# Phases of two key steps with eight slots, two streams of half contractions and an MLP that goes chunk by chunk, in a fused attention and MLP kernel

## The chip, the cores and the metric

The kernel runs on one core of a Trainium2 chip. The metric is the device time in microseconds (us) of one execution, lower is better; before the change the median of three runs is 1293.92 us (1293.52 to 1295.2).

## The reference

Per token a gate `g` mixes an attention output and an MLP output. The attention has 32 query heads of 16 channels that share one key and one value head; the MLP has a hidden width of 1792 and a squared ReLU. There are 2048 tokens of width 512, all in float32.

```python
g = sigmoid((x * gate_w).sum(-1, keepdims=True))
q = (x @ wq).reshape(B, S, 32, 16).transpose(0, 2, 1, 3)
p = softmax(einsum("bhqd,bkd->bhqk", q, x @ wk) * 16 ** -0.5)
a = einsum("bhqk,bkd->bhqd", p, x @ wv).transpose(0, 2, 1, 3).reshape(B, S, 512) @ wo
h = relu(x @ w1 + b1) ** 2
b = h @ w2 + b2
out = g * a + (1 - g) * b
```

## The kernel before

**Numbers.** A float32 factor is cut into a rounded part `r` and a rest `l` (a *split*: two VectorE instructions, a cast L163 and a subtraction L164), and a product of two factors is three matrix products (`pairs`, L166). A matmul with a contraction of 128 is done as two halves of 64 rows that run side by side on the array, each into a PSUM bank of its own; `mm2` (L173) issues the two halves of a term in a row. Such a pair is called a *slot* here. VectorE adds the two banks when the last term is in. There are three banks for this (`mp`), four for scores (two tiles of two banks, `sp`) and one for the context (`acc`).

**Attention.** The tokens are cut into four chunks `c` of 512, the heads into eight groups of four: 32 iterations `it` (chunk by chunk). An iteration goes over 16 key tiles of 128 (*steps*). A step is two *half-steps* of 256 queries: `scores` (L496) issues two matmuls side by side (L503) and the exponential of their 128x1024 results on ScalarE (L507), into a buffer `e`. `context` (L510) multiplies the exponentials with the values and a column of ones (L518): four matmuls side by side in 32 columns each, with 512 queries where both halves of a step are at hand, otherwise with 256. `finish` (L535) copies the sums out; `unpack` (L186) moves them by two DMAs of SP's queue, `q_load` (L355) loads the queries of the next iteration by six more, and `pieces` (L553) divides them on VectorE in four parts of 128 columns (`divide`, L526) and stores `oTs`.

**The other work.** `work` (L605) is a generator that yields between slots: 14 tiles of query projection (`qproj`; the first two are done ahead of the attention), the MLP, and the output projection. The MLP (`mlp`, L438) goes over pairs of hidden tiles `f`, and within a pair over the four chunks: `first` (L440) makes a hidden tile (12 slots; bias, square and split on VectorE, L449 to L451), `second` (L456) adds two hidden tiles to the result `res[c]` (four units of 6 slots, two evictions L468 each). All `x` chunks and all of `res` stay in SBUF; each weight tile is loaded (`w_load`, 512 KB for both layers) and split (`w_split`) once, in three buffers.

**The order is written out by hand.** `phase` (L657) issues one piece of division, one *chore* of the list `chores` (a load, a split, or nothing), and then scores of three half-steps with six slots among them (`FULL`), or of two half-steps with two slots (`LIGHT`, three in the last unit); then follows the context of the phase before. `by_now` (L429) pulls chores forward when a unit needs the weight they split. Which kind comes next is what the generator yields. An iteration of 32 half-steps makes eleven full phases, one of which has two half-steps. All engines work through their own queue in this order.

Of the kernel before, what the change touches and what calls it, by code (L numbers as in the profile page):

```python
# [21 lines left out]
KT = D // 128  # L22
# [12 lines left out]
FULL, LIGHT = 3, 2  # L35
# [4 lines left out]
C_ID, C_BLK, C_A, C_ONE, C_SEL, C_N = 0, 128, 136, 137, 138, 155  # L40
# [15 lines left out]
def exact_shift(tc, k_aug, v_ext, qs, oTs, gms, cs, wo, o_load, o_split, outproj, unpack):  # L56
# [63 lines left out]
    with tc.tile_pool(name="gx", bufs=1) as gx, tc.tile_pool(name="gy", bufs=4, space=PSUM) as gy:  # L120
        wof = gx.tile([128, KT, D], F32, name="wof")
        wor = gx.tile([128, KT, D], F32R, name="wor")
        wol = gx.tile([128, KT, D], F32R, name="wol")
        nc.sync.dma_start(wof, wo.rearrange("(t p) n -> p t n", p=128))
        nc.vector.tensor_copy(wor, wof)
        nc.vector.tensor_tensor(wol, wof, wor.bitcast(F32), OP.subtract)
        for c in range(NC):
            orr, orl, todo = o_split(gx, c, o_load(gx, c))
            for f in todo:
                f()  # L130
            for _ in outproj(gx, gy, c, orr, orl, wor, wol, "gm"):
                pass
# [3 lines left out]
def mix_kernel(ctx: ExitStack, tc: tile.TileContext, xT, wkv, wq, wo, w12, b1, b2, cst, out):  # L136
# [3 lines left out]
    gms = dram.tile([2, 16, 128], F32, name="gms")  # L140
    keep = ctx.enter_context(tc.tile_pool(name="keep", bufs=1))
# [18 lines left out]
    res = []  # L160
# [12 lines left out]
    def mm2(pa, pb, terms, per):  # L173

        for i, (a, b) in enumerate(terms):
            for ps, rows in ((pa, slice(0, 64)), (pb, slice(64, 128))):
                nc.tensor.matmul(ps, a[rows], b[rows], start=i == 0, stop=i == len(terms) - 1)  # L179
            if i < len(terms) - 1:  # L180
                if i % per == per - 1:
                    yield FULL if per > 3 else LIGHT
                elif i % per == 2:
                    yield 0

# [5 lines left out]
    def o_load(xpool, c, n=KT):  # L191
        oT = xpool.tile(sh, F32, name="oT", tag=("xr0", "xl0")[c % 2])
        nc.sync.dma_start(oT[:, :n], oTs[c * NG:c * NG + 2 * n].rearrange("(t u) d n -> (u d) t n", u=2))
        return oT

    def o_split(xpool, c, oT):
        orr = xpool.tile(sh, F32R, name="orr", tag=("xr2", "xr3")[c % 2])
        orl = xpool.tile(sh, F32R, name="orl", tag=("xl2", "xl3")[c % 2])
        return orr, orl, [lambda t=t: split(orr[:, t], orl[:, t], oT[:, t]) for t in range(KT)]

    def outproj(pool, pp, c, orr, orl, wor, wol, tag):
        for j in range(4):
            cols = slice(j * 128, (j + 1) * 128)
            ps = [pp.tile([128, D], F32, name=tag) for _ in range(2)]
            yield from mm2(*ps, [u for t in range(KT) for u in
                                 pairs(orr[:, t, cols], orl[:, t, cols], wor[:, t], wol[:, t])], 2)
            s = 4 * c + j
            ot = pool.tile([128, D], F32, name="ot", bufs=2)
            nc.vector.scalar_tensor_tensor(ot, ps[0], g[:, s:s + 1], res[c][:, j], op0=OP.mult, op1=OP.add)  # L209
            nc.vector.scalar_tensor_tensor(ot, ps[1], g[:, s:s + 1], ot, op0=OP.mult, op1=OP.add)  # L210
            nc.gpsimd.dma_start(out[s * 128:(s + 1) * 128], ot)
            yield LIGHT
# [6 lines left out]
    with fast, tc.tile_pool(name="at", bufs=1) as at, \  # L219
# [5 lines left out]
        wkvf = at.tile([128, KT, 128], F32, name="wkvf", tag="wf")  # L225
# [3 lines left out]
        def x_load(c):  # L229
            for a in range(2):  # L230
                if a == 0:
                    both = at.tile([128, KT, CH], F32, name="xf", tag="e", bufs=3)
# [14 lines left out]
        b2t = at.tile([128, D], F32, name="b2t")  # L247
        nc.sync.dma_start(b2t, bass.AP(tensor=b2.tensor, offset=b2.offset, ap=[[0, 128], [1, D]]))
        nc.sync.dma_start(b1t, b1.rearrange("(t p) -> p t", p=128))

        blk = at.tile([128, 8], BF, name="blk")
        ones = at.tile([96, 128], BF, name="ones")
        wkr = at.tile([128, KT, 128], F32R, name="wkr", tag="w1r", bufs=3)
        wkl = at.tile([128, KT, 128], F32R, name="wkl", tag="w1l", bufs=3)
# [7 lines left out]

        def run(gen):
            while True:
                try:
                    next(gen)
                except StopIteration as e:
                    return e.value
# [8 lines left out]
        def kv(c):  # L277
            ps = mp.tile([128, CH], F32, name="mm")
            mm(ps, [t for k in range(KT) for t in pairs(wkr[:, k], wkl[:, k], xr[c][:, k], xl[c][:, k])])
            kvs = at.tile([128, CH], F32, name="kvs", tag="h", bufs=2)  # L280
            kb = at.tile([128, CH], F32R, name="kb", tag="of", bufs=8)
            sq = at.tile([96, CH], BF, name="sqk", tag="sq", bufs=2)
# [29 lines left out]
        def qproj(c, t, early=False):  # L312
            cols = slice(t * 128, (t + 1) * 128)
            terms = [u for k in range(KT) for u in
                     pairs(wqr[:, k, cols], wql[:, k, cols], xr[c][:, k], xl[c][:, k])]
            qr = at.tile([128, CH], F32R, name="qr", tag="of", bufs=8)
            ql = at.tile([128, CH], F32R, name="ql", tag="of", bufs=8)
            sq = at.tile([128, CH], BF, name="sq", bufs=2)
            if early:
                q = mp.tile([128, CH], F32, name="mm")  # L320
                mm(q, terms)
                nc.scalar.activation(qr, q, AF.Copy)
            else:
                ps = [mp.tile([128, CH], F32, name="mm") for _ in range(2)]
                yield from mm2(*ps, terms, 6)
                q = at.tile([128, CH], F32, name="qf", tag="of", bufs=8)
                nc.vector.tensor_copy(q, ps[0])
                nc.vector.tensor_tensor(q, q, ps[1], OP.add)
                nc.vector.tensor_copy(qr, q)
            nc.vector.tensor_tensor(ql, q, qr.bitcast(F32), OP.subtract)  # L330
            nc.vector.tensor_tensor(sq, qr.bitcast(F32), qr.bitcast(F32), OP.mult)
# [5 lines left out]
            return it, sq  # L337

        def qnorm(it, sq):
            p8 = mp.tile([128, CH], F32, name="mm")  # L340
            nc.tensor.matmul(p8[:8], blk, sq, start=True, stop=True)  # L341
            nrm = at.tile([8, CH], F32R, name="nrm", bufs=2)
            tmp = at.tile([8, CH], F32, name="tmp", tag="n")
            nc.vector.tensor_copy(tmp, p8[:8])
            root(nrm, tmp, tmp)
            o = qs[it, 0, DH]
            nc.sync.dma_start(bass.AP(tensor=o.tensor, offset=o.offset,
                                      ap=[[KS * 2 * CH, 4], [CH, 2], [1, CH]]), nrm.bitcast(F32))
            done.update((it, it + 1))
# [13 lines left out]
        wf, w1, w2 = {}, {}, {}  # L363

        def w_load(f):
            wf[f] = at.tile([128, 1024], F32, name="wf")
            nc.sync.dma_start(wf[f], w12[f])

        def w_split(f, half):

            dst = (w1, w2)[half]
# [397 lines left out]
```

## Time and profile before

| of the profiled execution | |
|---|---|
| its time | 1294.1 us |
| span from first to last instruction | 1292.2 us |
| TensorE matmuls (PE), busy | 1263.2 us, 98% |
| ScalarE (ACT), busy | 1030.8 us, 80% |
| VectorE (DVE), busy | 625.8 us, 48% |
| mean granted TensorE clock | 0.992 |
| DMA | 57.36 MB, mean 44 GB/s |

The profile was taken on the core itself. PE is TensorE's matmuls, PEld its weight loads, which lie beside them; SPq is the queue from which SyncE issues DMAs. A line of a view gives the engine, the line of the kernel, output and inputs by the program's names, the shape, how many there were, their busy time and the mean of one in ns; "idle" or a bracket is the time that the engine stood just ahead, and what ended it. Matmuls overlap, so their busy time says little of how many more would fit; starts of neighbouring instructions say more.

### The profile page before, as it was taken

To read this page: it belongs to the slowest core of one execution; us is meant where nothing else is said; L and a number is where in the kernel's file an instruction comes from. 1 tells how busy PE (TensorE), PEld (TensorE's weight loads), DVE (VectorE), ACT (ScalarE), POOL (GpSimd) and SP (SyncE) were. 2 spreads that over 40 slices of the span, in tenths; PEclk is the share of its full clock that TensorE was granted. 3 is DMA by queue.
4 is the path that set the end of the run, shared out by engine and by line. 5 is a ranking of instruction groups with operands and counts; after the bars stand their busy time and mean duration, and the time that the engine had idled before them with its cause. 6 is when DMAs were issued, how large, how long until landed. Compare 5 with 4: busy or idle time off the path is not lost.

```text
span 1292.2 us, 25244 instructions
## 1 busy us (share of the span) xinstructions
PE 1263.2 (98%) x10722; PEld 642.5 (50%) x10722; DVE 625.8 (48%) x1117; ACT 1030.8 (80%) x1084; POOL 58.9 (5%) x66
## 2 busy tenths in 40 slices
PE   8899999999999999999999999999999999999996
PEld 5455555555555555555555555555554433322232
DVE  6567855546555464464645547457580304020212
ACT  5677787777877777777777777877779999999984
POOL 2010150200000000000000000000000000000000
PEclk9899999999999999999999999999999999999998
DMA  6233311000101000110011000121001120110100
GB/s 207 79 92 90 93 39 38 30 14 34 38 22 47 15 27 26 39 46 15 16 38 38 30 14 33 38 88 62 18 13 39 46 78 31 53 38 22 54 1 35
DMA packets 29661, 57.36 MB, mean 44 GB/s; under 512 B 8936, under 2 KB 10600, under 8 KB 29544
## 3 DMA queue, kind: packets, MB, share of 16 engines
q1 hardware_dynamic: 23288, 44.40, 10.6%
q0 software_dynamic: 5968, 10.77, 2.6%
q8 instruction: 86, 1.41, 0.4%
q10 hardware_dynamic: 288, 0.52, 0.1%
q14 instruction: 31, 0.25, 0.1%
HBM read 31.02 MB, written 16.78 MB: 37 GB/s over the span
## 4 chain that ended last, share of the span: by engine, by line
PE 91%; ACT 5%; DVE 1%; DMA 1%; issue 1%; SPq 0%; ACTq 0%; DVEq 0%
PE acc L518 35%; PE mm L179 30%; PE s L503 23%; ACT e L507 5%; PE mm L171 1%; DMA xf<-in_xT 1%; DMA qa<-qs 1%; PE mm L341 0%; PE s L171 0%; DMA qs<-nrm 0%; DVE res L468 0%; PE mm L568 0%; PE s L300 0%; ACT accs L545 0%; DVE al L541 0%
## 5 line engine op out<-in xcount | busy, mean ns | idle before, releaser
L507 ACT ACTIVATE e<-s 128x1024 f32<-128x1024 f32 x1024 | 998.5, 1024 | 228.4 <-PE s L503 178.9
L518 PE MATMUL acc<-e,v_ext 128*32 128x512 f32 (+1 forms) x5128 | 524.8, 514 | 0.7 <-ACT e L507 0.7
L503 PE MATMUL s<-qa,k_aug 49*128 49x512 f32 x2048 | 452.5, 439 | 13.0 <-ACT e L507 9.5
L503 PEld LDWEIGHTS s<-qa,k_aug 49*128 49x128 f32 x2048 | 193.7, 184 | 329.7 <-ACT e L507 217.2
L518 PEld LDWEIGHTS acc<-e,v_ext 128*32 128x32 f32 x5128 | 129.2, 108 | 223.4 <-issue 194.3
L468 DVE SCALAR_TENSOR_TENSOR res<-mm,omg,res 128x512 f32<-128x512 f32 x224 | 168.2, 751 | 132.7 <-PE mm L179 119.6
L449 DVE TENSOR_SCALAR h<-mm,b1t 128x512 f32<-128x512 f32 x56 | 42.0, 751 | 208.1 <-PE mm L179 208.1
L179 PE MATMUL mm<-w2r,hr 64*128 64x512 f32 x448 | 91.5, 397 | 0.1
L179 PE MATMUL mm<-w2l,hr 64*128 64x512 f32 x448 | 90.3, 392 | 0.0
L179 PE MATMUL mm<-w2r,hl 64*128 64x512 f32 x448 | 89.7, 390 | 0.0
L179 PE MATMUL mm<-xr,w1l 64*128 64x512 f32 x448 | 88.7, 393 | 0.0
L179 PE MATMUL mm<-xr,w1r 64*128 64x512 f32 x448 | 88.2, 391 | 0.0
L179 PE MATMUL mm<-xl,w1r 64*128 64x512 f32 x448 | 88.2, 390 | 0.0
L209 DVE SCALAR_TENSOR_TENSOR ot<-mm,g,res 128x512 f32<-128x512 f32 x12 | 9.0, 752 | 120.2 <-PE mm L179 120.2
L532 DVE RECIPROCAL n<-n 128x128 f32<-128x128 f32 x60 | 57.2, 953 | 2.1
L529 DVE TENSOR_SCALAR n<-lc 128x128 f32<-128x128 f32 x60 | 13.3, 221 | 75.8 <-DMA lc<-accs 75.3
L179 PEld LDWEIGHTS mm<-w2r,hl 64*128 64x128 f32 x448 | 43.4, 184 | 10.4
L179 PEld LDWEIGHTS mm<-w2l,hr 64*128 64x128 f32 x448 | 43.8, 187 | 8.9
L561 POOL DMA_DIRECT2D oTs<-oc x15 | 8.3, 551 | 871.2 <-DVE oc L533 861.1
L179 PEld LDWEIGHTS mm<-xl,w1r 64*128 64x128 f32 x448 | 42.5, 186 | 9.7
L179 PEld LDWEIGHTS mm<-w2r,hr 64*128 64x128 f32 x448 | 44.2, 187 | 5.9 <-DVE res L468 0.9
L179 PEld LDWEIGHTS mm<-xr,w1l 64*128 64x128 f32 x448 | 41.9, 184 | 9.5
(127 smaller groups left out, 776.6 us busy)
## 6 DMA issues: line engine op xcount, KB each, us to landing
qa<-qs SPq DMA_DIRECT2D x128, 64.0 KB
wf<-in_w SPq DMA_DIRECT2D x14, 512.0 KB
qa<-qs SPq DMA_DIRECT2D x64, 68.0 KB
xf<-in_xT SPq DMA_DIRECT2D x8, 512.0 KB
qs<-qr SPq DMA_DIRECT2D x16, 256.0 KB
oc<-accs SPq DMA_DIRECT2D x30, 128.0 KB
lc<-accs SPq DMA_DIRECT2D x30, 128.0 KB
oTs<-oc POOLq DMA_DIRECT2D x15, 256.0 KB, 2.3
```

What stands on the lines that cost most here:

```text
L171: nc.tensor.matmul(ps, a, b, start=first and i == 0, stop=last and i == len(terms) - 1)
L179: nc.tensor.matmul(ps, a[rows], b[rows], start=i == 0, stop=i == len(terms) - 1)
L209: nc.vector.scalar_tensor_tensor(ot, ps[0], g[:, s:s + 1], res[c][:, j], op0=OP.mult, op1=OP.add)
L449: nc.vector.tensor_scalar(h, ps[0], b1t[:, f:f + 1], None, op0=OP.add)
L468: nc.vector.scalar_tensor_tensor(res[c][:, j], p, omg[:, s:s + 1], res[c][:, j], op0=OP.mult, op1=OP.add)
L503: nc.tensor.matmul(s[:, r].rearrange("p (a n) -> p a n", a=2), k_aug[rows, kt * 128:(kt + 1) * 128], qa[it][rows, :, cols], start=True, st ...
L507: nc.scalar.activation(es[u // 2][:, :, cols], s.rearrange("p r (a n) -> p (r a) n", a=2), AF.Exp, scale=SCALE)
L518: nc.tensor.matmul(acc[h * 32:(h + 1) * 32, cols], v_ext[:, i % NK], es[i][:, h % 2 * 2 + h // 2, cols], start=(i % NK == 0), stop=(i % NK ...
L529: nc.vector.tensor_scalar(n[:, cols], l[:, cols], L_MIN, L_MAX, op0=OP.max, op1=OP.min)
L532: nc.vector.reciprocal(n[:, cols], n[:, cols])
L561: nc.gpsimd.dma_start(oTs[it - 1:it + 1].rearrange("u d n -> (u d) n"), o)
```

## The change

It does six things.

1. A full phase has four half-steps (two whole steps) and eight slots, a light one two half-steps and two or three slots. Which one comes is computed from the slots that are left (`plan`), no longer from what the generator yields: full phases while more than one slot per half-step is left, then light ones. That makes 174 full phases and then 164 light ones. The context always has 512 queries; `e` has four buffers instead of three.
2. `stream` takes the place of `mm2`: the upper half of the contraction runs five slots behind the lower (`LAG`), across the borders of units. A slot still issues one matmul of each half, now of different terms or units, and a bank is taken only when its half begins.
3. The MLP goes chunk by chunk. Hidden tiles come in groups of 4, 4, 3 and 3 of a chunk, and a unit of the second layer sums a whole group in PSUM: 12 or 9 slots for two evictions.
4. Every weight tile is loaded and split once per chunk, 256 KB at a time, with one buffer for the loaded tile of each layer: `w_split` of a tile issues the load of the next. First-layer splits have two buffers, second-layer splits five. The split of a first-layer weight becomes a chore when the tile two ahead of it is evicted; those of the second layer when its group is summed.
5. `wo` and the attention output are split into buffers that chunks 2 and 3 of `x` gave up, so these chunks are loaded and split again; `res` has two buffers and goes to DRAM for the rarely taken second path.
6. A phase pops two chores when more than three are waiting, a division comes every phase instead of every second, query norms are done four at a time, and the second query tile moves from ahead of the attention into the stream.

```diff
-FULL, LIGHT = 3, 2
+GROUPS = (0, 1, 2, 3), (4, 5, 6, 7), (8, 9, 10), (11, 12, 13)
+FULL, LIGHT = 4, 2
+LAG = 5
...
+    def stream(units, pp):
+        late = []
+        def follow(keep):
+            if len(late) > keep:
+                late.pop(0)()
+        for unit in units:
+            if unit is None:
...
+            terms, outs, tag = unit
+            banks = [pp.tile([128, CH], F32, name=tag)]
+            def product(i, half, terms=terms, outs=outs, banks=banks, tag=tag):
+                if len(banks) == half:
+                    banks.append(pp.tile([128, CH], F32, name=tag))
+                a, b = terms[i]
+                rows = slice(64 * half, 64 * half + 64)
+                nc.tensor.matmul(banks[half], a[rows], b[rows], start=i == 0, stop=i == len(terms) - 1)
+                if i == len(terms) - 1:
+                    outs[half](banks[half])
+            for i in range(len(terms)):
+                late.append(lambda i=i, p=product: p(i, 1))
+                product(i, 0)
+                follow(LAG)
+                yield 1
...
+        def w_load(half, n):
+            if n < NC * NF:
+                wf[half][n] = at.tile([128, 512], F32, name=f"w{half + 1}f")
+                nc.sync.dma_start(wf[half][n], w12[n % NF, :, half * 512:half * 512 + 512])
+        def w_split(half, n):
+            if n < NC * NF:
+                ws[half][n] = [at.tile([128, 512], F32R, name=f"w{half + 1}{x}", bufs=(2, 5)[half]) for x in "rl"]
+                split(*ws[half][n], wf[half][n])
+                w_load(half, n + 1)
...
+        def hidden(c, f, hs):
+            n = c * NF + f
+            by_now(ws[0], n)
+            by_now(x, c)
...
+            def second(p):
+                hr, hl = hs[f] = ring[n % 5]
+                nc.vector.tensor_tensor(h[0], h[0], p, OP.add)
+                nc.vector.scalar_tensor_tensor(h[0], h[0], 0.0, h[0], op0=OP.max, op1=OP.mult)
+                split(hr, hl, h[0])
+                later(w_split, 0, n + 2)
+                if f == NF - 1 and c < 2:
+                    x_again(c + 2)
...
+        def summed(c, fs, hs):
...
+                def second(p, s=s, part=part, j=j):
+                    first(p, s, part)
+                    if j == 3:
+                        for f in fs:
+                            later(w_split, 1, n0 + f + 5)
...
+            for c in range(NC):
+                for fs in GROUPS:
+                    hs = {}
+                    for f in fs:
+                        yield hidden(c, f, hs)
+                        o_ready(c)
+                        if f == fs[0] and prev:
+                            yield from summed(*prev)
+                            if prev[1][-1] == NF - 1 and c > 1:
+                                yield from projection(c - 2)
+                    prev = c, fs, hs
...
+        def o_ready(c):
+            if c == 0 and not wos:
...
+                chores.extend([load] + [lambda: None] * 3)
+                for t in range(KT):
+                    chores.append(lambda t=t: split(wos[0][:, t], wos[1][:, t], wof[0][:, t]))
+            if c > 0:
+                ask(c - 1)
...
+            for _ in range(2 if len(chores) > 3 else 1):
+                if chores:
+                    chores.pop(0)()
+            if us:
+                scores(us.pop(0))
+            for i in range(1, slots + 1):
+                if not next(lazy, None):
+                    break
+                left -= 1
+                if i % 3 == 0 and us and slots > 3:
+                    scores(us.pop(0))
...
+        def plan(u):
+            if left > early + max(total - u - 40, 8) and u % FULL == 0:
+                return range(u, min(u + FULL, total)), 8
+            return range(u, min(u + LIGHT, total)), 3 if left > total - u else 2
```

**TensorE, one full phase of the second layer.** Before (`s` are scores, `mm` products, two to a slot, `acc` the context):

```order
L503 MATMUL s<-qa,k_aug 128x512 x2
L179 MATMUL mm<-w2r,hr 128x512 x2
L179 MATMUL mm<-w2l,hr 128x512 x2
L179 MATMUL mm<-w2r,hl 128x512 x2
L503 MATMUL s<-qa,k_aug 128x512 x2
L179 MATMUL mm<-w2r,hr 128x512 x2
L179 MATMUL mm<-w2l,hr 128x512 x2
L179 MATMUL mm<-w2r,hl 128x512 x2
L503 MATMUL s<-qa,k_aug 128x512 x2
L518 MATMUL acc<-e,v_ext 32x512 x4
L518 MATMUL acc<-e,v_ext 32x256 x4
```

After, from behind the first score of a phase (`hr` now names both parts of the hidden tile):

```order
L206 MATMUL mm<-w2l,hr 128x512
L206 MATMUL mm<-w2r,hr 128x512 x4
L206 MATMUL mm<-w2l,hr 128x512
L579 MATMUL s<-qa,k_aug 128x512 x2
L206 MATMUL mm<-w2l,hr 128x512
L206 MATMUL mm<-w2r,hr 128x512 x4
L206 MATMUL mm<-w2l,hr 128x512
L579 MATMUL s<-qa,k_aug 128x512 x2
L206 MATMUL mm<-w2l,hr 128x512
L206 MATMUL mm<-w2r,hr 128x512 x3
L579 MATMUL s<-qa,k_aug 128x512 x2
L594 MATMUL acc<-e,v_ext 32x512 x8
```

A phase has grown from three scores and six slots to four scores and eight slots, and its context from one and a half steps to two.

**VectorE where `wo` is split.** Before, one split (`wor`, `wol`) stood in a phase, with evictions (`res`) between:

```order
L163 CAST wor<-wof 128x512
L164 TENSOR_TENSOR wol<-wof,wor 128x512
L468 SCALAR_TENSOR_TENSOR res_1660<-mm,omg,res_1660 128x512 x2
L163 CAST wor<-wof 128x512
L164 TENSOR_TENSOR wol<-wof,wor 128x512
L468 SCALAR_TENSOR_TENSOR res_1660<-mm,omg,res_1660 128x512 x2
```

After, at hidden tile 2 of chunk 0 (`w2f`, `w1f` are loaded weights, `big` holds the hidden tile before its split):

```order
L170 CAST w2r<-w2f 128x512
L171 TENSOR_TENSOR w2l<-w2f,w2r 128x512
L492 TENSOR_SCALAR big<-mm,b1t 128x512
L170 CAST wor<-wof 128x512
L171 TENSOR_TENSOR wol<-wof,wor 128x512
...
L170 CAST w1r<-w1f 128x512
L171 TENSOR_TENSOR w1l<-w1f,w1r 128x512
L496 TENSOR_TENSOR big<-big,mm 128x512
```

All four splits of `wo` (the dots are three of them) now stand in a row ahead of the split of the weight that hidden tile 2 is multiplied with.

**VectorE in a group of hidden tiles.** Before, the split of a first-layer weight stood well ahead of its use, behind the second layer's evictions:

```order
L468 SCALAR_TENSOR_TENSOR res_1662<-mm,omg,res_1662 128x512 x2
L163 CAST w1r<-wf 128x512
L164 TENSOR_TENSOR w1l<-wf,w1r 128x512
L449 TENSOR_SCALAR h<-mm,b1t 128x512
L450 TENSOR_TENSOR h<-h,mm 128x512
L451 SCALAR_TENSOR_TENSOR h<-h 128x512
```

After, at hidden tiles 5 to 7 of chunk 1:

```order
L492 TENSOR_SCALAR big<-mm,b1t 128x512
L170 CAST w2r<-w2f 128x512
L171 TENSOR_TENSOR w2l<-w2f,w2r 128x512
L496 TENSOR_TENSOR big<-big,mm 128x512
L497 SCALAR_TENSOR_TENSOR big<-big 128x512
L170 CAST hr<-big 128x512
L171 TENSOR_TENSOR hr<-big,hr 128x512
L492 TENSOR_SCALAR big<-mm,b1t 128x512
L170 CAST w2r<-w2f 128x512
L171 TENSOR_TENSOR w2l<-w2f,w2r 128x512
L170 CAST w1r<-w1f 128x512
L171 TENSOR_TENSOR w1l<-w1f,w1r 128x512
```

Two more splits of second-layer weights stand just ahead of these rows; the split of `w1f`, the weight of tile 7, has moved behind four splits of the second layer and the evictions of tiles 5 and 6.

More of the change, by code (lines that the diff above doesn't have):

```diff
@@ L53, in constants, with exact_shift @@
     return c
[L56 removed]
+def exact_shift(tc, k_aug, v_ext, qs, oTs, gms, ress, cs, wo, split, outproj, stream, unpack):
     nc = tc.nc
@@ L310, in root, with q_write @@
             nc.vector.tensor_copy(dst, tmp)
[L312 to L331, printed above, removed]
+        def q_write(c, t, qr, ql, early=False):
             it = c * NG + 2 * t
@@ new lines, in ask, with load, part @@
+        def ask(c, n=KT):
+            if c in asked or any((c, t) not in complete for t in range(n)) or c > len(asked):
+                return
+            if c and not used[c - 1]:
+                return
+            asked.add(c)
+            tiles = []
+            def load():
+                tiles.extend((keep.tile(sh, F32, name="oT", tag="r2"), keep.tile(sh, F32R, name="orr", tag="r3"),
+                              xp.tile(sh, F32R, name="orl", tag="xl3")))
+                nc.sync.dma_start(tiles[0][:, :n], oTs[c * NG:c * NG + 2 * n].rearrange("(t u) d n -> (u d) t n", u=2))
+            def part(t):
+                oT, orr, orl = tiles
+                split(orr[:, t], orl[:, t], oT[:, t])
+                if t == n - 1:
+                    osp[c] = orr, orl
+            chores.extend([load] + [lambda: None] * 2)
+            for t in range(n):
+                later(part, t)
```

445 lines of the change are left out of this document (217 added, 228 removed).

## The prediction

> **What bounds the kernel now.** I read the page first, then the groups of instructions, then the timeline of single phases, then who waits for whom.
>
> ```profile
> PE 1263.2 (98%) x10722; PEld 642.5 (50%) x10722; DVE 625.8 (48%) x1117; ACT 1030.8 (80%) x1084; POOL 58.9 (5%) x66
> PE acc L518 35%; PE mm L179 30%; PE s L503 23%; ACT e L507 5%; PE mm L171 1%; DMA xf<-in_xT 1%; DMA qa<-qs 1%; PE mm L341 0%; PE s L171 0%; DMA qs<-nrm 0%; DVE res L468 0%; PE mm L568 0%; PE s L300 0%; ACT accs L545 0%; DVE al L541 0%
> DVE h L449 <- PE mm L179: 208.1, 55, 5.8
> PEld mm L179 <- DVE res L468: 0.9, 2, 0.6
> ```
>
> The chain that ended last is TensorE for 88% (context, slots, scores). VectorE waits for TensorE (208.1 us for first-layer tiles alone), TensorE for VectorE next to never: 0.9 us in two waits. So the price of a phase is read from the starts of TensorE's instructions. First a full phase of six slots, then a light one of two:
>
> ```profile
> 604.48 1.50 PE L518 MATMUL acc<-e,v_ext 128*32 128x256 f32 x16
> 605.91 0.50 PE L503 MATMUL s<-qa,k_aug 49*128 49x512 f32 x2
> 608.19 1.06 PE L518 MATMUL acc<-e,v_ext 128*32 128x512 f32 x8
> 609.19 0.50 PE L503 MATMUL s<-qa,k_aug 49*128 49x512 f32 x2
> 1045.76 0.50 PE L503 MATMUL s<-qa,k_aug 49*128 49x512 f32 x2
> 1046.88 1.07 PE L518 MATMUL acc<-e,v_ext 128*32 128x512 f32 x8
> 1047.88 0.50 PE L503 MATMUL s<-qa,k_aug 49*128 49x512 f32 x2
> ```
>
> The full phase goes from 605.91 to 608.19 (2.28 us, three scores and six slots), the light one from 1045.76 to 1046.88 (1.12 us, two and two). Five more things cost 1.16 us: 0.232 each, whether score or slot, and four of them would be 0.93, so 0.19 us of a phase is change-over. A context of one step takes 1.00 (608.19 to 609.19), one of a step and a half 1.43 (604.48 to 605.91): half a step more is 0.43. The light phase takes 2.12 in all. For whole iterations of 32 half-steps the issues on SP's queue give the period, first with full phases, then with phases without a slot:
>
> ```profile
> 609.95 0.47 SPq L188 DMA_DIRECT2D oc<-accs  x1
> 611.16 2.46 SPq L360 DMA_DIRECT2D qa<-qs  x6
> 650.19 0.47 SPq L188 DMA_DIRECT2D oc<-accs  x1
> 1173.98 0.47 SPq L188 DMA_DIRECT2D oc<-accs  x1
> 1206.30 0.47 SPq L188 DMA_DIRECT2D oc<-accs  x1
> ```
>
> 40.24 us with eleven full phases, 32.32 us (2.02 for two half-steps) without slots, where the exponentials set the pace.
>
> **The phases.** Before, 252 full phases (28 for queries, 112 for each layer) are 22.9 iterations, 921.9 us and 733 half-steps. Of the other 291, 84 light phases have slots (72 of the output projection, 12 of its last part): 178.1 us; the other 61.5 take 124.2. Sum 1224 us. After, a full phase has 12 things: 2.28 + 3 x 0.232 = 2.98, and a context of two steps, 1.00 + 2 x 0.43 = 1.86: 4.84 us for four half-steps; the old iteration takes 40.24 / 8 = 5.03 for as many, with a quarter slot more. 173 of them are 837 us; the 164 light phases, nearly all with two slots, 348. Sum 1185. The first phase has no context to go with it and eight slots at the slow clock of the start, which I put at 2 us. That is 37 us less; the drain of five lagging halves behind the last context takes 1 back. **Without any new wait the profiled 1294.1 us become 1258 us.** ScalarE doesn't forbid it:
>
> ```profile
> 606.53 2.86 ACT L507 ACTIVATE e<-s 128x1024 f32<-128x1024 f32 x3 [0.92 <-PE s L503]
> ```
>
> Three exponentials in a row take 2.86, so four need 3.8 of the 4.84 us, and the fourth buffer of `e` gives them room. That each half begins its bank late costs nothing by itself: a bank is evicted (0.75 us) while at least five slots run.
>
> **VectorE's new work.** The durations:
>
> ```profile
> L468 DVE SCALAR_TENSOR_TENSOR res<-mm,omg,res 128x512 f32<-128x512 f32 x224 | 168.2, 751 | 132.7 <-PE mm L179 119.6 <-DVE res L468 0.9
> L449 DVE TENSOR_SCALAR h<-mm,b1t 128x512 f32<-128x512 f32 x56 | 42.0, 751 | 208.1 <-PE mm L179 208.1
> L164 DVE TENSOR_TENSOR hl<-h,hr 128x512 fp32r<-128x512 f32 x56 | 38.8, 693 | 1.9
> L451 DVE SCALAR_TENSOR_TENSOR h<-h 128x512 f32<-128x512 f32 x56 | 38.8, 692 | 1.9
> L450 DVE TENSOR_TENSOR h<-h,mm 128x512 f32<-128x512 f32 x56 | 38.5, 688 | 6.2 <-PE acc L518 0.5
> L163 DVE CAST hr<-h 128x512 fp32r<-128x512 f32 x56 | 25.1, 448 | 1.9
> L163 DVE CAST w1r<-wf 128x512 fp32r<-128x512 f32 x14 | 5.9, 418 | 1.5 <-DMA wf<-in_w 1.5
> L164 DVE TENSOR_TENSOR w1l<-wf,w1r 128x512 fp32r<-128x512 f32 x14 | 9.7, 692 | 0.5
> L532 DVE RECIPROCAL n<-n 128x128 f32<-128x128 f32 x60 | 57.2, 953 | 2.1
> ```
>
> Evictions of the second layer fall from 224 to 128: 96 x 0.75 = 72 us saved. Weight splits rise from 28 to 112: 84 x (0.42 + 0.69) = 93 us added, and two chunks of `x` are split again, 8 x 1.11 = 9. So VectorE's sum hardly moves, and on average it is half idle. What counts is the order. A first-layer tile's chain is 0.75 for the lower half, then 0.69 + 0.69 + 0.45 + 0.69 = 2.5 us; a part of a division is about 1.8 (0.95 of it the reciprocal). A split waits for its own load, the load is issued only when the split before has emptied the one buffer, and everything behind it on VectorE waits too, evictions among them. The load's price:
>
> ```profile
> oTs<-oc POOLq DMA_DIRECT2D x15, 256.0 KB, 2.3
> 1220.15 0.39 SPq L193 DMA_DIRECT2D oT<-oTs  x1
> 1224.60 0.43 DVE L163 CAST orr<-oT 128x512 fp32r<-128x512 f32 x1 [7.06 <-DMA oT<-oTs]
> ```
>
> 256 KB landed in 2.3 us from another queue; with SP's issue I take 2.7 (bounds 2.3, and 4.45 as 768 KB took from issue to use). From 2.7 and 4.45, 1 MB takes 5.3.
>
> **Where TensorE then waits.** Take tile 7 of chunk 1, the shape that recurs. Zero is the start of the phase in which tile 5 ends. VectorE's last eviction ahead is done at -2.1. Then: split of `w2` to -1.0; its load to 1.7, the next split to 2.7; eviction of tile 5's lower half to 3.5; third split, its load in at 5.4, to 6.5; tile 5's chain to 9.05; tile 6's lower half to 9.8; fourth split to 10.9; cast of tile 7's weight to 11.35. TensorE wants that weight with the first slot two phases on, at 9.68 + 0.33 = 10.0. It waits 1.4 us, and 0.2 for the rest `l`: 1.6. A division's part in that stretch adds 1.8 each time. Eight places have this shape: chunk 0 tile 7 (3.6), the end of chunk 0 (0.7), chunk 1 tiles 3, 7, 11 and end (3.3, 1.9, 1.6, 2.7), chunk 2 tile 7 and end (1.9, 2.7); tile 3 of chunks 2 and 3 wait 2.1 each behind divisions. **22 us** together. Three are longer:
>
> - Chunk 0 tile 11, about **9 us**: the issue of the six `qa` loads stands on SP's queue ahead of the second load (0.47 + 0.60 + 2.46 and the copy before it put it at 4.4 instead of -1.0), so tile 9's eviction holds up a bank by 3.6, and the chain behind, with a division, costs the rest.
> - Chunk 0 tile 2, about **18 us**: with zero at the start of its phase, `qa` has been issued at 4.4, the load for the next `w2` split lands at 7, that split ends at 8.0; only then SP issues the next load and that of `wo`, 1 MB behind 256 KB: 14.5; four splits to 18.9, the cast to 19.3. TensorE wants it at 1.5.
> - Chunk 2 tile 11, about **11 us**: four splits and three loads in a row end 0.7 into its phase; the load of the attention output to 6.4, four splits to 10.8, the cast to 11.2, wanted at 0.3.
>
> The sum is 60 us, with nothing to hide it: TensorE is the bound there and its order is fixed. With loads at 2.3 it would be some 52; with loads at 4.45, which three times the bytes took, some 100: I stay near the lower end. If the queues run further apart than I walked them, the eight short waits go, and 38 are left.
>
> **The clock** adds to that:
>
> ```profile
> 36.00:38.00 2.00, 0.00 (x0) 0.00 (x0) 1.97 (x4) 0.00 (x0) 0.00 (x0) 0.71 0.24 44
> 38.00:40.00 2.00, 1.23 (x5) 0.54 (x5) 1.29 (x6) 1.12 (x2) 0.00 (x0) 0.50 0.89 292
> 40.00:42.00 2.00, 1.88 (x8) 1.18 (x10) 0.00 (x0) 1.96 (x3) 0.00 (x0) 0.50 0.49 164
> 42.00:44.00 2.00, 2.00 (x14) 1.56 (x12) 0.00 (x0) 1.32 (x2) 0.00 (x0) 0.58 0.27 88
> ```
>
> After the start's wait of some 2.5 us TensorE ran at 0.50 for about 5.5 us (38 to 43.6), which costs half of them, 2.75. For the two longest waits that is 5.5 us; for the short ones I take nothing. The Trainium skill (TensorE: Matmul & The Clock Gate, "What's actually happening") says that the clock halves after an idle window of about 3.4 us and needs a busy one of about 3.4 us to come back: an estimate by that page is 1.7 us a wait, 3.4 in place of 5.5.
>
> **Sum:** 1294.1 - 36 + 60 + 5.5 = 1323.6, about **1324 us**, 2.3% slower. The median of the runs is 0.2 below the profiled time, which I leave aside.
>
> **The rivals.**
>
> 1. *The waits are hidden* (0.14). VectorE is idle half of the time; if it runs so far ahead that weights are split before TensorE comes, only the phases count: 1258 us. For it speaks that VectorE waited for TensorE everywhere; against it that loads with one buffer can't run ahead, and that `wo` is asked for where it is needed. It decides below 36 us of waits.
> 2. *Half of the waits* (0.12): the short ones go, 38 and a little clock stay: 1258 + 38 = 1296; with the long ones also shortened 1285 to 1300.
> 3. *The clock falls after every wait* (0.06): 13 waits x 2.75 = 36 in place of 5.5: 1354. The window from 36 to 44 shows it for one idle stretch of about 2.5 us; most of mine are shorter. The skill's page, with its window of 3.4 us, would have only waits as long as that do it.
> 4. *Longer phases save nothing* (0.04): if the 0.19 of change-over grows with the phase, or two streams side by side run less well than two halves of one term, a phase stays at 5.03 less the quarter slot, 4.97: 173 x 0.13 = 22 more, 1346. Both halves are already issued alternately now, which speaks against it.
>
> My forecast has 0.64. The range 1275 to 1350 holds it with its bounds on the load, the upper part of rival 2 and part of 4; below it lies most of rival 1, above it rival 3. Faster by over 0.2% (what a measurement of this kernel can tell, 2.6 us): rival 1 and half of 2, 0.20. Same 0.06. Slower 0.74.
>
> **What would show it.** The full phases: starts of scores 4.84 us apart where nothing waits; light ones 2.12. The waits: TensorE's weight loads with `w1r` or `w1l` from VectorE as releaser, some 60 us in a dozen places, one of about 18 near 160 us and one of about 11 near 770 us, each with the granted clock at 0.5 behind it; VectorE waiting for `w2f`, `wof` and `oT`. I am wrong if TensorE's idle time for VectorE stays under 36 us, or if the phases aren't 4.84.

## The result

1397.2 us median of four runs (1392.2 to 1400.9) against 1294.4: 1.0792 of the time before, 95% interval 1.0754 to 1.0830. Slower, as forecast, but by 103 us and not by 30. The profiled execution has a span of 1396.9 us (before: 1292.2).

The page of the changed kernel: the busy times, the granted clock in 40 slices, and the chain that ended last.

```profile
PE 1274.1 (91%) x9702; PEld 629.6 (45%) x9702; DVE 632.2 (45%) x1173; ACT 1016.1 (73%) x1083; POOL 58.7 (4%) x68
PEclk9799969998999999999999999999999999999998
PE 74%; DVE 12%; DMA 11%; SPq 1%; issue 1%; ACT 1%; DVEq 0%; ACTq 0%
```

VectorE's sum has hardly moved (625.8 before), as forecast. New is that 23% of the chain are VectorE and DMA (2% before): TensorE now waits for a split, and the split for its load. The clock is reduced most in slice 6 (175 to 210 us), then in slice 2, the start (35 to 70 us), and in slice 10 (314 to 349 us); before, no slice but the second and the last stood below 9. The list of waits, for TensorE and then for VectorE (total, times, longest):

```profile
PE mm L206 <- DVE w1r L170: 73.7, 18, 23.1
PE mm L206 <- DVE big L492: 10.9, 3, 7.9
PE mm L206 <- DVE res L520: 6.8, 2, 6.4
DVE w2r L170 <- DMA w2f<-in_w: 81.6, 25, 13.1
DVE orr L170 <- DMA oT<-oTs: 24.5, 3, 12.3
DVE w1r L170 <- DMA w1f<-in_w: 23.8, 4, 8.9
```

`big L492` and `res L520` are evictions: the long ones, 7.9 and 6.4 us, also come from VectorE, which stood at a load with the eviction queued behind. How much TensorE idled in all is read from its busy time in one long stretch, from 40 us to 30 us before the end, of before and then of after:

```profile
40.00:1262.00 1222.00, 1212.45 (x10485) 613.51 (x10487) 589.86 (x1049) 998.70 (x1042) 49.80 (x57) 1.00 0.12 40
```

```profile
40.00:1366.00 1326.00, 1226.62 (x9461) 602.23 (x9461) 596.91 (x1104) 984.65 (x1043) 53.58 (x62) 0.96 0.18 58
```

Idle: 1222.00 - 1212.45 = 9.6 us before, 1326.00 - 1226.62 = 99.4 after. That is 90 us. The same stretch in windows of 1 us, each window's busy time weighted with how far its clock lies below 1, gives the time that TensorE worked at half speed: 3.6 us before, 66.3 after. If work at half speed takes twice as long (a context of two steps takes 3.63 us at 0.50 and 1.92 at 1.00, both shown below), half of the difference, 31 us, is lost. So of 104.7 us more span, 90 are idle time, 31 the clock, and what is left, the phases and the start, has become 16 us shorter. This last figure is a remainder. The busy time, less half of what ran at half speed, says nearly the same: 1210.7 us before and 1193.5 after, 17 less.

The phases, where nothing waits: the starts of two contexts and of the scores behind them, on TensorE, and one iteration on SP's queue.

```profile
640.48 1.92 PE L594 MATMUL acc<-e,v_ext 128*32 128x512 f32 x16
642.33 0.50 PE L579 MATMUL s<-qa,k_aug 49*128 49x512 f32 x2
...
645.38 1.92 PE L594 MATMUL acc<-e,v_ext 128*32 128x512 f32 x16
647.24 0.50 PE L579 MATMUL s<-qa,k_aug 49*128 49x512 f32 x2
```

```profile
904.74 0.47 SPq L221 DMA_DIRECT2D oc<-accs  x1
943.84 0.47 SPq L221 DMA_DIRECT2D oc<-accs  x1
```

The context of two steps takes 1.85 (forecast 1.86), the twelve scores and slots 3.05 (2.98), the iteration 39.10: 4.89 a phase, against 4.84 forecast and 5.03 before.

**A place that was not forecast so.** SP's queue, VectorE and the DMA engines around 330 us, in the changed kernel:

```profile
322.25 2.46 SPq L406 DMA_DIRECT2D qa<-qs  x6
324.81 18.79 SPq L414 DMA_DIRECT2D w2f<-in_w  x4
```

```profile
332.22 0.43 DVE L170 CAST w2r<-w2f 128x512 fp32r<-128x512 f32 x1 [13.08 <-DMA w2f<-in_w]
333.29 0.74 DVE L492 TENSOR_SCALAR big<-mm,b1t 128x512 f32<-128x512 f32 x1
335.87 0.43 DVE L170 CAST w2r<-w2f 128x512 fp32r<-128x512 f32 x1 [1.84 <-DMA w2f<-in_w]
```

```profile
324.00:328.00 4.00, 2.16 (x17) 0.62 (x9) 0.00 (x0) 1.72 (x2) 0.00 (x0) 1.00 0.40 114
328.00:332.00 4.00, 0.00 (x0) 0.00 (x0) 0.00 (x0) 0.00 (x0) 0.00 (x0) 0.66 0.06 24
```

The load issued at 324.81, just behind the six `qa` pieces, is used at 332.22: 7.4 us for 256 KB. The next, with the split done at 333.37, is used at 335.87: 2.5 us, nearly the 2.7 that I took. The last columns of the windows say what differs: from 328 to 332 the DMA engines' share is 0.06, as much as one engine of sixteen, and they move 24 GB/s. Such a stretch behind a transfer is called its *tail* here. The eviction `big L492` waits behind that split, and TensorE for the eviction, 7.9 us. The kernel before has the same tail (its window from 615 to 619 us reads 0.08 and 30 GB/s), but there nothing that was wanted at once stood behind it.

The long places that were forecast are there too: 23.1 us at chunk 0 tile 2 (forecast 18), 7.9 + 2.2 at chunk 0 tile 11 (9), 11.6 at chunk 2 tile 11 (11). In the first of them a load had the `qa` pieces ahead of it too: issued at 179.09, it was used at 184.35, 5.3 us later.

### The profile page after: what moved, and what is told of

Same layout as the page of the kernel before. It is cut to its first block, busy times and chain, and to the rows that moved or that the text cites. A ratio compares the mean times of both kernels' runs of the same rounds, so it can differ in the third digit from the quotient of the medians.

```text
span 1396.9 us, 23321 instructions
## 1 busy us (share of the span) xinstructions
PE 1274.1 (91%) x9702; PEld 629.6 (45%) x9702; DVE 632.2 (45%) x1173; ACT 1016.1 (73%) x1083; POOL 58.7 (4%) x68
## 4 chain that ended last, share of the span: by engine, by line
PE 74%; DVE 12%; DMA 11%; SPq 1%; issue 1%; ACT 1%; DVEq 0%; ACTq 0%
PE acc L594 29%; PE mm L206 25%; PE s L579 19%; DMA w2f<-in_w 6%; DVE w2l L171 2%; DMA w1f<-in_w 2%; DMA oT<-oTs 2%; DVE w2r L170 1%; PE mm L178 1%; DVE n L608 1%; DVE big L497 1%; DVE big L496 1%; DVE hr L171 1%; DVE big L492 1%; DVE res L520 1%
## 5 line engine op out<-in xcount | busy, mean ns | idle before, releaser
L594 PE MATMUL acc<-e,v_ext 128*32 128x512 f32 x4096 | 516.9, 608 | 0.0
L579 PE MATMUL s<-qa,k_aug 49*128 49x512 f32 x2048 | 464.3, 442 | 10.8 <-DMA qa<-qs 10.4
L206 PE MATMUL mm<-w2r,hr 64*128 64x512 f32 x896 | 213.0, 394 | 6.8 <-DVE res L520 6.8
L520 DVE SCALAR_TENSOR_TENSOR res<-mm,omg,res 128x512 f32<-128x512 f32 x128 | 95.9, 750 | 265.5 <-PE mm L206 265.5
L206 PE MATMUL mm<-w2l,hr 64*128 64x512 f32 x448 | 160.1, 395 | 0.0
L206 PEld LDWEIGHTS mm<-w2r,hr 64*128 64x128 f32 x896 | 130.1, 188 | 23.2 <-DVE res L520 7.5
L206 PE MATMUL mm<-xragain,w1r 64*128 64x512 f32 x224 | 84.0, 415 | 35.4 <-DVE w1r L170 32.5
L206 PE MATMUL mm<-xragain,w1l 64*128 64x512 f32 x224 | 83.3, 405 | 0.0
L206 PE MATMUL mm<-xlagain,w1r 64*128 64x512 f32 x224 | 82.9, 411 | 0.0
L206 PEld LDWEIGHTS mm<-xr,w1r 64*128 64x128 f32 x224 | 43.9, 199 | 57.0 <-DVE w1r L170 44.0
L206 PEld LDWEIGHTS mm<-xragain,w1r 64*128 64x128 f32 x224 | 43.4, 194 | 43.8 <-DVE w1r L170 35.9
L170 DVE CAST w2r<-w2f 128x512 fp32r<-128x512 f32 x56 | 24.2, 432 | 81.6 <-DMA w2f<-in_w 81.6
L492 DVE TENSOR_SCALAR big<-mm,b1t 128x512 f32<-128x512 f32 x56 | 42.0, 750 | 39.8 <-PE mm L206 37.6
```

The lines of the kernel that those rows point to most:

```text
L170: nc.vector.tensor_copy(r, src)
L206: nc.tensor.matmul(banks[half], a[rows], b[rows], start=i == 0, stop=i == len(terms) - 1)
L492: nc.vector.tensor_scalar(h[0], p, b1t[:, f:f + 1], None, op0=OP.add)
L520: nc.vector.scalar_tensor_tensor(part, p, omg[:, s:s + 1], part, op0=OP.mult, op1=OP.add)
L579: nc.tensor.matmul(s[:, r].rearrange("p (a n) -> p a n", a=2), k_aug[rows, kt * 128:(kt + 1) * 128], qa[it][rows, :, cols], start=True, st ...
L594: nc.tensor.matmul(acc[h * 32:(h + 1) * 32, cols], v_ext[:, i % NK], es[i][:, h % 2 * 2 + h // 2, cols], start=(i % NK == 0), stop=(i % NK ...
```

## The experiments

Theory A, after the comparison: the stalls have separate causes (a late load behind `qa`, the order of VectorE's chores, one buffer for loaded weights), and the slow clock behind them is a price of its own. Rivals: one cause for all (loads alone, or the amount of VectorE's work), and a loss in the phases themselves.

**The `qa` piece of seventeen rows as sixteen and one**

```
-Q_ROWS = (0, 0, DH), (DH, 0, DH), (RS, DH, KS)
+Q_ROWS = (0, 0, DH), (DH, 0, DH), (RS, DH, 2 * DH), (RS + DH, 2 * DH, KS)
```

> Only the seventeen-row piece of each qa load is issued as sixteen rows and one row. Theory A (one DMA engine carries the two 68 KB pieces alone; the trace shows 25 GB/s, a sixteenth of the 390 seen when all run, for 4 to 5 us after each qa load, and whatever stands behind qa on SP's queue lands only then): the 25 GB/s tails go, loads issued behind qa land 3 to 4 us after their issue in place of 7.4 to 9, the stalls at 334, 479, 523 and 775 us (7.9, 6.4, 4.5, 4.9) lose 4 us each or go, and with their clock the time falls by 25 to 45 us, to 1350-1372. Theory B (the loads are late because many bytes are under way, or since SP issues slowly): the tails stay, two more issues per iteration cost SP 0.8 us, and the time stays within 5 us of 1397.

1367.2 us, 1.0559 [1.0542, 1.0577] of before: 30 us off. SP's queue, VectorE and the DMA engines at the same place (it comes 8.4 us earlier):

```profile
313.86 3.61 SPq L406 DMA_DIRECT2D qa<-qs  x8
317.58 14.18 SPq L414 DMA_DIRECT2D w2f<-in_w  x4
```

```profile
320.21 0.43 DVE L170 CAST w2r<-w2f 128x512 fp32r<-128x512 f32 x1 [9.47 <-DMA w2f<-in_w]
```

```profile
320.00:322.00 2.00, 0.00 (x0) 0.00 (x0) 1.75 (x3) 0.00 (x0) 0.00 (x0) 0.50 0.00 0
```

The tail is gone and the load is used 2.6 us after its issue in place of 7.4, although SP now takes 3.6 us for the pieces. Theory A in the time and in the stalls: 7.9, 6.4 and 4.9 us become 4.3, 2.1 and 2.0. But its "and with their clock" fails: TensorE still works 66 us at half speed, for stalls of 2 to 4 us are left. 5.8 of the 30 us come at the start, where the first iteration ends at 81.3 in place of 87.1: the first scores wait for `qa` too.

**The first-layer split at the front of the chores**

```
-                later(w_split, 0, n + 2)
+                chores.insert(0, lambda: w_split(0, n + 2))
```

> A first-layer weight's split is put at the front of the chores instead of at their end; nothing else. Theory A (the order of VectorE's work causes the long stalls: the split that TensorE wants stands behind other loads and splits): the stalls at 197, 842 and 1153 us (23.1, 11.6, 8.4) and the ten of 1 to 3 us go, those behind a late load (334, 479, 523, 775) stay; 55 to 65 us of idle time and 15 to 20 us of slow clock less: 1315-1330. Theory B (the loads are what is late, and the order only decides which instruction waits for them): the waits move to the evictions and second-layer splits, and the time stays above 1370.

1356.4 us, 1.0485 [1.0468, 1.0503]: 41 us off, between the two. TensorE's waits for `w1r` fall from 73.7 to 37.8 us. At chunk 0 tile 2 the stall of 23.1 becomes 6.1, not nothing: VectorE stands before it at a second-layer split whose load came behind the `qa` pieces (6.1 us there). So order was the larger single cause, but part of it was only handed on to the loads, which I had not counted.

**Two buffers for loaded second-layer weights** (the second one in the place of the second output tile)

```
-                w_load(half, n + 1)
+                w_load(half, wf[half][n])
...
-                    ots.extend((big[:, 0], big[:, 1]))
+                    ots.extend((big[:, 0], big[:, 0]))
+                    w_load(1, big[:, 1])
```

> A second buffer for loaded second-layer weights (it takes the place of the second output tile), so that each load has a whole split's time more. Theory A (the price is in the order, and loads matter only behind qa): VectorE's waits for w2f fall from 82 us to under 25, the short stalls and those at 270, 334, 391 and 441 shrink, 197 becomes about 18, 842 about 9, 1153 and 775 stay; 25 to 35 us of idle time and some 10 us of clock less: 1350-1365. Theory B (single-buffered loads are the whole cause): at or below 1320.

1367.3 us, 1.0570 [1.0542, 1.0597]: 30 us off, near A. VectorE's waits for second-layer loads fall from 81.6 to 24.8 us, but TensorE still waits 64.4 us for `w1r`: the loads with one buffer are not the whole cause.

**The weights not loaded and split again** (later tiles are multiplied with the weights of earlier ones)

```
-            if n < NC * NF:
+            kept = (2, 5)[half]
+            if n >= kept:
+                ws[half][n] = ws[half][n - kept]
+            elif n < NC * NF:
```

> Weights are loaded and split for two first-layer and five second-layer tiles alone; later tiles use these again (wrong weights: the work that goes is 105 loads and 105 pairs of split instructions). TensorE's work and order are unchanged; the loads and splits of wo, of the attention output and of x stay. Theory A (phases as forecast, all the rest of the loss is waits for these splits and the slow clock behind them): 1262-1280, granted clock 0.985 or more. Theory B (part of the loss is in the phases themselves or in work that the change moved elsewhere): above 1300.

1302.5 us, 1.0072 [1.0055, 1.0089]: 95 us off, 22 above what A allowed, and still slower than before. What is left is not in the phases. TensorE idles 29.0 us and works 21.9 at half speed. The waits of this run on VectorE for loads that stayed:

```profile
DVE orr L170 <- DMA oT<-oTs: 25.5, 2, 13.5
DVE w2r L170 <- DMA w2f<-in_w: 18.9, 3, 6.6
DVE wor L170 <- DMA wof<-in_wo: 5.2, 1, 5.2
```

The 1 MB loads of `oT`, issued behind `qa` where an iteration ends, hold evictions up; the iteration with the first of them takes 46.9 us, most of its neighbours 39.1. My expectation had left these out. Both theories are partly wrong here: a stall needs no weight to be split again.

**The kernel before with sixteen and one rows**

> The kernel before, with the seventeen-row piece of each qa load issued as sixteen rows and one, as in the first run of this study, and nothing else. Theory A (the 25 GB/s tail costs only what stands behind qa and is wanted at once; before, that is the start alone, 3.3 us of waits for qa, with the slow clock behind): 3 to 6 us faster than before, 0.996 to 0.998 of it, by an earlier first iteration; later iterations stay at 40.2. Theory B (the tail costs bandwidth all along): every iteration gets shorter and the gain is over 10 us.

1290.0 us, 0.9966 [0.9955, 0.9977]. The first iteration ends at 80.25 in place of 84.10, later ones stay at 40.2. So the tail cost the old kernel 4 us, once, at the start. Theory A.

**The three edits together**

> The changed kernel with the three edits that were run alone: the seventeen-row piece as sixteen and one, first-layer splits at the front, two buffers for loaded second-layer weights. Alone they took 30, 41 and 30 us off 1397. Theory A (three separate causes, each stall belonging to one of them or to two in a row): at least the sum, 101 us: 1285-1300. Theory B (they shorten the same stalls, and a chain of splits on one engine remains): 1320 or above.

1297.9 us, 1.0024 [1.0012, 1.0035]: 99 us off, where the three alone sum to 101. Theory A, though "at least the sum" is missed by 2 us: the three edits hardly share a gain. Which stall each of them took isn't shown by a sum.

**The three edits, with more room behind the 1 MB loads**

```
-            chores.extend([load] + [lambda: None] * 2)
+            chores.extend([load] + [lambda: None] * 8)
```

(and the same for `wo`)

> As the run of the three edits together, and the splits of wo and of the attention output come eight phases' chores behind the issue of their 1 MB loads in place of two or three. Theory A (what is then left are the stalls at those loads: evictions behind 8 to 13 us waits for oT and wo, 6 to 8 us each, and the slow clock behind them): 15 to 25 us below the run without this, at 1265-1282, and below the kernel before. Theory B (TensorE's stalls there come from the amount of work on VectorE): within 5 us of the run without it.

1296.0 us, 1.0013 [1.0004, 1.0023]. Theory A fails: 2 us where I expected 15 to 25. The stalls that it meant were gone already: the run with the three edits has none there. With sixteen and one rows alone, the two at the `oT` loads had fallen from 6.4 and 8.4 us to 2.1 and 4.0, so the tails were the larger part of their price. What holds now stands on SP's queue and VectorE:

```profile
288.57 3.90 SPq L406 DMA_DIRECT2D qa<-qs  x8
292.58 0.37 SPq L416 DMA_DIRECT2D big<-in_w  x1
```

```profile
295.16 0.43 DVE L170 CAST w2r<-big 128x512 fp32r<-128x512 f32 x1 [6.13 <-DMA big<-in_w]
```

The split before ended at 286.5, but at 287.35 SP began with the two copies and eight pieces that an iteration's end brings, 5.2 us in all, and the load (`big` is its second buffer) came behind them.

**The weight loads on GpSimd's queue, and instead the `qa` loads there** (each with all the edits above)

```
-                nc.sync.dma_start(into, w12[n % NF, :, half * 512:half * 512 + 512])
+                nc.gpsimd.dma_start(into, w12[n % NF, :, half * 512:half * 512 + 512])
```

```
-                    nc.sync.dma_start(q[64 * r + row:64 * r + row + b - a].bitcast(F32), qs[it, r, a:b])
+                    (nc.gpsimd if it else nc.sync).dma_start(q[64 * r + row:64 * r + row + b - a].bitcast(F32), qs[it, r, a:b])
```

> The run with the three edits and room, and the weight loads issued on GpSimd's queue in place of SP's. Theory A (what is left are loads that stand behind two copies and eight qa pieces, 4.5 us of issue, on SP's queue where an iteration ends just before a weight is wanted): the stalls at 302, 462 and 705 us (5.0, 2.5, 2.9, with half speed behind two or three of them; the iterations 47.1, 43.5 and 43.8 long in place of 39.1) go, 15 to 17 us: 1276-1283, the first version below the kernel before. Theory B (the qa pieces hold the DMA engines, whatever queue issues; or GpSimd's own waits take SP's place): within 4 us of 1296.

> The run with the three edits and room, and the qa loads of all iterations but the first issued on GpSimd's queue (weights stay on SP's). Theory A (SP's issue time ahead of the weights): as the other run, 1277-1285, since only the two copies, 1.1 us, stay ahead of a weight. Theory B (the transfers themselves compete): the loads that fall right behind qa still land late, within 4 us of 1296.

1281.6 us, 0.9905 [0.9890, 0.9920], and 1284.8, 0.9926 [0.9914, 0.9939]: both below the kernel before, both as A says. The first one's long stretch, and TensorE's largest waits in it:

```profile
40.00:1248.00 1208.00, 1193.73 (x9459) 586.32 (x9461) 594.54 (x1104) 981.00 (x1042) 112.25 (x172) 1.00 0.22 64
```

```profile
PE s L581 <- DMA qa<-qs: 5.8, 2, 4.9
PE mm L206 <- DVE w1r L170: 8.0, 10, 1.4
```

14.3 us idle, 0.8 us at half speed. This run is the check on the phases: it has the changed kernel's phases and almost no waits, and it is the fastest of all. Its busy time, less half of what ran at half speed, is 1193.3 us, as in the changed kernel (1193.5).

**The lag of the upper halves** (on the run that uses its weights again)

```
-LAG = 5
+LAG = 0
```

> As the run that uses its weights again (wrong weights, 105 loads and splits left out), with the upper halves directly behind the lower ones (lag 0 in place of 5). Theory A (the lag is what lets a unit end inside a phase: with three banks the next unit's upper half needs the bank whose eviction, 0.75 us, has just begun): TensorE waits some 0.7 us at 150 to 220 unit ends, 1302 becomes 1390-1460. Theory B (the lag adds nothing, as the wait hides behind scores and contexts): within 10 us of 1302.

1363.1 us, 1.0531 [1.0514, 1.0549]: 61 us above the run with the lag. The direction is A's, the size some two thirds of its low end. TensorE's waits for evictions, new at unit ends:

```profile
PE mm L206 <- DVE res L523: 26.1, 36, 4.9
PE mm L206 <- DVE big L495: 24.0, 28, 4.3
```

They come at 64 places, not at 150 or more, 50 us in these two rows. Such a wait costs more than the idle time that it shows: the 63 full phases at full clock that hold one take 5.94 us on average, 0.60 of it idle, against 4.88 for most of those without. That is 1.06 each and 67 in all, more than the 61, since other waits became shorter. Against the old kernel, whose units ended where a phase ended and where TensorE waited 0.9 us for evictions, the lag can save no wait; here it is what lets a unit end inside a longer phase.

**The stalls filled with idle matmuls**

```
+            for _ in range(fillers.pop() if fillers else 0):
+                nc.tensor.matmul(banks[0], k_aug[:, :128], k_aug[:, :CH], start=True, stop=True)
...
+            fillers.append(FILL.get((c, f), 0))
```

> The changed kernel with idle matmuls (261 of 128 x 512, into the bank that the next unit starts in and overwrites) ahead of thirteen first-layer tiles that stall, each place's count set to its stall less 0.6 us at 0.232 us a matmul; all weights, splits, loads and their order stay as they are. Theory A (the slow clock behind a stall is a price of its own, half of 5 to 6 us of work per place): TensorE waits as long as before, now working, the clock stays at full speed behind the nine of these places that now show 0.5, and the time falls by nine times 2.75, 25 us, to 1370-1378, granted clock 0.97 or above. Theory B (what lies behind a stall is set by VectorE and ScalarE catching up, whatever TensorE's clock): the time stays within 4 us of 1397, or rises.

1384.1 us, 1.0699 [1.0675, 1.0723]: 13 us off, by adding work. That is well outside theory B's 4 us, but about half of what A expected (25) and 6 us above its range. The granted clock rises from 0.954 to 0.981, the time at half speed falls from 66.3 to 23.7 us. The fill of the longest stall, and the first context behind it, in this run and then in the changed kernel:

```profile
176.04 22.07 PE L204 MATMUL mm<-k_aug 128*128 128x512 f32 x96
...
199.63 1.92 PE L600 MATMUL acc<-e,v_ext 128*32 128x512 f32 x16
```

```profile
196.66 0.79 PE L206 MATMUL mm<-xr,w1r 64*128 64x512 f32 x1 [23.14 <-DVE w1r L170]
...
199.52 3.63 PE L594 MATMUL acc<-e,v_ext 128*32 128x512 f32 x16
```

The context takes 1.92 us in place of 3.63. So the clock is a price of its own, with its size less sure than that it exists: of the 21 us that half of 42.6 makes, the fill brought 13. It also added 2.5 us (41.3 idle and 261 x 0.232 filled, against 99.4), and the remaining 5 or 6 I can't place.

## Why the prediction was right in sign and wrong in size

The sum had three terms: phases -36, waits +60, clock +5.5. The runs give -16, +90 and +31 (the last by the half price, less by the fill; the first is the remainder).

- **Phases.** The mechanism held: a phase of eight slots and two steps of context costs less than two old ones for the same work. The size was off. 4.89 in place of 4.84 is 173 x 0.05 = 8 us. The first iteration ends 3 us later than before (87.1, before 84.1), which I had not counted: TensorE waits 10.4 us for its first `qa`, before 3.3. The other 9 us stay open; the query iterations, which take 41 to 43 us even in the fastest version, hold some of them.
- **Waits at the places I had walked.** 23.1 + 10.1 + 11.6 for the three long ones (forecast 18 + 9 + 11), and some 21 us for a dozen short ones of 1.0 to 2.6 us (forecast 22 in ten): 66 against 60. Here the order of VectorE's chores was the right way to look, and the run with the first-layer splits in front shows that it was a cause. That the sum came so near is partly luck. At chunk 0 tile 11 I had 3.6 us at the held bank and the rest in the chain behind it; it was 7.9 and 2.2, because a load took 7.4 us. And at chunk 0 tile 2 the 5.3 us load is part of the 23.1.
- **Waits that I had not seen.** 6.4 us at 479 (an eviction behind the load of `oT`), 4.5 at 523, 4.9 at 775 (first-layer loads behind `qa`), 8.4 at 1153 (`oT` again): 24 us. The step that failed is the load's price: "with SP's issue I take 2.7 (bounds 2.3, and 4.45 ...)". For a load that stands right behind `qa` it was 7.4, 7.7 and 7.6 us (issued at 324.81, 514.61 and 766.80), above my upper bound; the 1 MB of `oT` behind `qa` took 10.3 and 10.0 (issued at 466.47 and 1135.87), and 5.5 where no `qa` stood ahead (831.36); I had 5.3 for 1 MB. The row on which that bound rested had no `qa` ahead of it; with 4.45 for every load I had put the waits at some 100, nearer to the 90 than my 60. I had priced SP's issue time for those pieces and not what they leave on the DMA engines. The Trainium skill (DMA: Bandwidth & Descriptors, "Why a DMA increments its semaphore by 16 and not by 1") states it: a copy uses the largest number of engines, up to 16, that divides the slowest dimension of both its sides, so seventeen rows go to one engine. The trace agrees (0.06 of the engines, 24 GB/s), and so does the run with sixteen and one.
- **The clock.** "for the short ones I take nothing" is the other step that failed. The 5.5 us at half speed that I read off the start is about right (66 us in twelve places is 5.5 each), but it follows some stalls of 1.5 to 2.6 us as well. My third rival, with 36 us for thirteen waits, was near in this term; I gave it 0.06. Its reason, that the clock falls after every wait, doesn't hold: behind six of the stalls between 1.5 and 2.9 us it did not (the table at the end).

The first two rivals, waits hidden or halved, fell. The fourth, that longer phases save nothing, fell too: the versions almost without stalls are faster than the kernel before, and a full phase takes 4.89 us, not the 4.97 of that rival. The three measured terms make up 1397 by construction, since the first is the remainder of the other two; what stands beside them as a check is the 17 us less of full-speed work, in the changed kernel and in the run with its weight loads on GpSimd's queue alike.

## What to carry to other kernels

Price a transfer with what its queue has ahead of it, on the DMA engines and not only at the issue, and look at the engines' share in the windows behind each transfer: a long 0.06 is what one engine of sixteen working alone looks like, and here a piece of seventeen rows made it, while sixteen rows and one did not. When a bound engine begins to wait for an engine that is half idle, ask in which order that one has its work; a sum of busy time says nothing on it. Count with TensorE's stalls a slow stretch behind them: here it followed every stall of 4.5 us or more and five of the eleven between 1.5 and 2.9 us, and by the half price it added a third to what the stalls cost.

## What the runs showed of the hardware

The clock after a stall of TensorE of 1.5 us or more, all in the changed kernel between 100 and 1366 us (stall, then the granted clock behind it):

| stall, us | at, us | clock behind it |
|---|---|---|
| 1.51 | 1028.9 | 0.50 for about 7 us |
| 1.58, 1.83 | 511.7, 889.3 | 1.00 |
| 2.10 | 626.5 | 0.50 for about 3 us |
| 2.21, 2.22, 2.31 | 166.7, 343.6, 579.9 | 1.00 |
| 2.26, 2.57, 2.62 | 440.9, 269.9, 391.3 | 0.50 for 3 to 6 us |
| 2.86 | 119.2 | 1.00 |
| 4.5 to 23.1, seven stalls | | 0.50 for 3 to 6.5 us |

Two rows of TensorE at 0.50 and at 1.00, with 0.79 and 0.50 us for the first matmul:

```profile
626.51 0.79 PE L206 MATMUL mm<-xragain,w1r 64*128 64x512 f32 x1 [2.10 <-DVE w1r L170]
```

```profile
343.64 0.50 PE L206 MATMUL mm<-xr,w1r 64*128 64x512 f32 x1 [2.22 <-DVE w1r L170]
```

Between 1.5 and 2.9 us the length does not decide. The Trainium skill (TensorE: Matmul & The Clock Gate, "What's actually happening") has a free-running window of about 3.4 us, which fits a result that depends on where a stall falls; but it asks for a whole idle window, and a stall of 1.51 us can't fill one, so there the measurement speaks against the page. In the 3.41 us ahead of the clock's fall at 1029.04, TensorE was busy for 1.90 us. What decides between 1.5 and 2.9 us stays open.
